# The first 1024 rows of a second Fourier mixing layer take their products with the hidden DFT matrices as seven turned block products

## Chip, cores and metric

One core of one Trainium2 chip. The metric is the device time of one execution in microseconds (us), lower is better. Of the engines, TensorE (PE) multiplies, VectorE (DVE), ScalarE (ACT) and GpSimd (POOL) work on tiles, and SyncE (SP) issues most DMAs; POOL issues the stores.

## The reference

Two mixing layers and two feed-forward layers in turn on x of 2048 rows and 512 columns, fp32, each on a layer-normed input and with a residual:

```python
def _A_ref(x, dft_seq_re, dft_seq_im, dft_hid_re, dft_hid_im):
    a = jnp.einsum("bsd,ed->bse", x, dft_hid_re)
    b = jnp.einsum("bsd,ed->bse", x, dft_hid_im)
    y = jnp.einsum("ts,bse->bte", dft_seq_re, a) - jnp.einsum("ts,bse->bte", dft_seq_im, b)
    return y

def _B_ref(x, w_gate, w_up, w_down):
    return (_gelu(x @ w_gate) * (x @ w_up)) @ w_down

x = x + _A_ref(_layernorm(x), dft_seq_re, dft_seq_im, dft_hid_re, dft_hid_im)
x = x + _B_ref(_layernorm(x), w_gate, w_up, w_down)
x = x + _A_ref(_layernorm(x), dft_seq_re, dft_seq_im, dft_hid_re, dft_hid_im)
x = x + _B_ref(_layernorm(x), w_gate, w_up, w_down)
```

The feed-forward width is 1792.

## The kernel before

**Arithmetic.** fp32 accuracy comes from splitting each operand into two fp32r tiles, hi and lo. `split` (L155) has ACT copy the source into hi (L157) and then DVE subtract hi from the source into lo (L159; for a negative operand L183 and L185). One product of 128x128 by 128x512 is then three matmuls (`mm3`, L214 to L216). The tiles of 128x512 live in 98 numbered slots (`sb`), taken in the order in which they came free; two wide tiles, `wide` (z) and `xwide` (x), can be lent out as four more slots each (`lend`).

**Layers.** Layers 0 and 2 mix (`mix`, L822), layers 1 and 3 are the feed-forward (`geglu`, L1269), done in two halves w = 0 and 1. A mixing layer multiplies first along the sequence, then by the hidden matrices wh. It works on four blocks b of 512 rows; the sequence product uses a seven-product scheme for 2 by 2 blocks, so that each block runs through stages: A11 and A12 for all four blocks first, and then for each block S2 (three interleaved chains, 24 steps of six matmuls, `six`, L988), S4 (two chains, 16 steps) and the products with wh. In S2 DVE also makes the sums of the raw DFT tiles (`make_s2`: one addition and two subtractions for every third item), in S4 one subtraction for every second.

**Products with wh.** In an unpaired block they are eight groups of four row tiles (`hid_groups`, L837; 12 matmuls a group). x is added by copying it into the four banks beforehand (`x_seeded`), and ACT copies the banks out (`x_out`). In layer 2 blocks 2 and 3 are a pair (`PAIRED`): seven forms P1 to P7, each with four operands k and two banks, six matmuls for each (`pair_product`, L910), with a prepared divided matrix wq. The result is turned, so DVE transposes it in 32 by 32 blocks and adds it into xwide or wide (`turned_into`, L812: the transpose is L815, the addition L197). For the first block of a pair P1 and P2 are done, for the second P7 and P4, and then come the twelve rest products of P6, P5 and P3 (`PAIR_REST`), which all add into one pair of banks:

```python
    def pair_rest(i):
        if sums_due:
            pair_sums()
        if i in (4, 5):
            first_sum(i - 4)
        pair_product(*PAIR_REST[i])
```

At each form's end DVE (or ACT, for P1, P2 and P7) reads the banks (`pair_ended`, L923). The operands of the forms come from `arrived` (L870) and `pair_sums` (L890, two operations of DVE for each k). For blocks 2 and 3 the twelve rest products go into the list `spare` and are taken one at a time between the products of the feed-forward layer (`beside_mix`, L1342).

**Order of the work.** All operands pass through one stream of items in the order of the products. `take` (L352) hands out the next item and splits up to seven items ahead (`AHEAD`), as far as what they are made from is there; loads run four items further (`RAW`):

```python
            if too_far(at) or make is not whole and at > n + AHEAD + stream["more"]:
                break
            if make is not whole and need and need not in cs and at > n:
                break
```

Side work is in `queue` (one at each step), `slow` (one at every few steps) and `chores` (spread over a block's products with wh; among them the norms of the next layer, `block_steps`, with their transposes at L740). A planner then orders each engine's instructions: in a planned time line it takes the ready instruction that comes first in the program. `behind` (L150) holds a split or a sum behind the newest read of a bank on its engine:

```python
    def behind(engine):
        return tc.issue_after(bank_read[engine].ins) if in_order[0] and engine in bank_read else ExitStack()
```

There are eight banks (`ps8`). DFT tiles `ws` are loaded at L337; the sums for the first two steps of block 3 are made ahead (`summed_ahead`).

Of the kernel before, what the change touches and what calls it, by code (L numbers as in the profile page):

```python
# [17 lines left out]
ND = D // P  # L18
# [25 lines left out]
MIXED = 4  # L44
PAIRED = {2: (2, 3)}
LATER = 3
LET = 5
# [6 lines left out]
def fnet_geglu(ctx: ExitStack, tc: tile.TileContext, x_in, ws, wh, wgu, wdn, wdc, whc, out):  # L54
# [409 lines left out]
    )  # L464
    PAIR_REST = [(name, k) for name in ("P6", "P5", "P3") for k in (2, 3, 0, 1)]
# [12 lines left out]
    def plan(layer):  # L478

        fore, steps = FORE[layer], []  # L480
        steps += [(b, "A11") for b in range(fore)] + [(b, "A12") for b in range(fore)]
        for b in range(NB):
            if b >= fore:
                steps += [(b, "A11"), (b, "A12")]
            if b in PAIRED.get(layer, ()):
                n = PAIRED[layer].index(b)
                steps += [(b, "S2"), (b, PAIR_EARLY[n]), (b, "S4"), (b, PAIR_LATE[n])]
            else:
                steps += [(b, "S2"), (b, EARLY_HID), (b, "S4"), (b, MID_HID), (b, LATE_HID)]
        return steps  # L490
# [23 lines left out]
    def mix_items(layer):  # L514
# [3 lines left out]
        for b, what in plan(layer):  # L518
# [17 lines left out]
            elif what == "S4":  # L536
                for i, k in skewed(2):
                    if layer and (b, k) in wss and i == 0:
                        raw(plain, wss[b, k][3])
                    elif i == 0:  # L540
                        raw(make_s4(layer, b, k), a12[k])
                    else:
                        raw(plain, a22[k])
            elif b in PAIRED.get(layer, ()):
# [277 lines left out]
    def mix(layer):  # L822
        hid, sums, chores, hid_left = {}, {}, [], [0]

        def chores_at(b):
            if b == NB - 3:
# [39 lines left out]

        paired = PAIRED.get(layer, ())
        xu, xv, pair_banks, kept_p, pair_wide, late_v, sums_due = {}, {}, {}, {}, {}, {}, []

        def arrived(b, m, c):  # L870
            if b not in paired:
                return
            t = cs.pop((m, c))
            if b == paired[0]:
                (xv if m else xu)[c] = t
                cs["P2" if m else "P1", c] = t
                return
# [19 lines left out]

        def pair_wide_load(n):
# [3 lines left out]
            moved(pair_wide[n], xs[layer, paired[n]], lambda v, rows: nc.sync.dma_start(v, rows))  # L902

        def pair_out(n):
            moved(pair_wide[n], xs[layer + 1, paired[n]], lambda v, rows: nc.gpsimd.dma_start(rows, v))

# [153 lines left out]
        def s2(b):  # L1060
            last = b == NB - 1
            if b == 0:
                lend("z")
# [39 lines left out]
        def s4(b):  # L1103
            last = b == NB - 1
            if b == NB - 4:
                sb.reclaim("z")
            if paired and b == paired[0] - 1:
                sb.reclaim("x")
# [160 lines left out]
    def geglu(w, layer):  # L1269
# [72 lines left out]
        def beside_mix(n):  # L1342
            run = spare.pop(0) if spare and (layer > 1 or n >= 1) else None
            if run:
# [62 lines left out]

        if layer == 1 and w and PAIRED:
            jobs = [weight_steps(k, whc, whd) for k in range(ND)]
            jobs = [(load, runs) for load, runs in jobs] + [(load, [run]) for load, run in map(summed_ahead, range(SUMMED))]  # L1410
# [376 lines left out]
```

## Time and profile before

| | us |
|---|---|
| three runs | 1596.59, 1596.60, 1599.89 |
| median | 1596.60 |
| span of the profiled execution | 1596.4 |
| PE busy | 1590.0 |
| DVE busy | 1169.2 |
| ACT busy | 891.6 |
| POOL busy | 294.9 |

The profile's only time for its own execution is the span, from the first to the last instruction; it stands 0.2 us below the median. The page is one execution taken by the hardware profiler. Lines such as L159 are lines of the kernel, and of a helper where a helper issues the instruction. A group of instructions is written as output<-inputs, its form, its count, its busy time and the mean length of one, and the idle time before it with what ended that. In a row of a window the columns are the stretch, its length, and for PE, PEld, DVE, ACT and POOL the busy time and in brackets the number of instructions, then the granted clock, the DMA share and GB/s. An engine's instructions overlap a little, so their mean length is more than the distance of their starts.

### The profile page before, as it was taken

The page shows a single profiled execution, that of the slowest core. Times are in us where ns is not written, and L with a number is a line of the kernel's source. Part 1 is how long each engine was busy: PE and PEld are TensorE (multiplying, and loading weights), DVE is VectorE, ACT ScalarE, POOL GpSimd, SP SyncE. Part 2 cuts the span into 40 slices and gives each one's busy share as a digit, 9 for nine tenths or more (in the row PEclk, how much of TensorE's full clock was granted, in tenths as well). Part 3 has the DMA queues.
Part 4 walks back from the last instruction along what each step waited for, and adds up shares of the span by engine and source line. Part 5 has one row for each costly group of instructions (what it writes and reads, how often), then busy time and mean ns, then how long its engine had stood idle before and what let it go on. Part 6 is the DMA issues. An engine that isn't in the chain of part 4 may idle for free.

```text
span 1596.4 us, 22835 instructions
## 1 busy us (share of the span) xinstructions
PE 1590.0 (100%) x6984; PEld 1311.2 (82%) x6984; DVE 1169.2 (73%) x2030; ACT 891.6 (56%) x1731; POOL 294.9 (18%) x505
## 2 busy tenths in 40 slices
PE   9999999999999999999999999999999999999999
PEld 6888888888888888888888888888888888888887
DVE  7997878888689794665879767778895557844574
ACT  8955465755777553666657535556553565333460
POOL 4122111251456101330040000101301000000000
PEclk9999999999999999999999999999999999999999
DMA  9898888996988999997895876878978958895445
GB/s 352 289 336 310 292 319 274 359 315 201 324 317 321 285 319 295 332 363 239 288 303 177 272 248 215 272 239 256 254 258 275 284 182 253 300 291 175 133 145 158
DMA packets 244058, 431.75 MB, mean 270 GB/s; under 512 B 29344, under 2 KB 68512, under 8 KB 242912
## 3 DMA queue, kind: packets, MB, share of 16 engines
q1 hardware_dynamic: 214128, 337.21, 66.2%
q0 software_dynamic: 27120, 90.99, 15.7%
q10 hardware_dynamic: 2688, 2.10, 0.5%
q8 instruction: 55, 0.90, 0.2%
q14 instruction: 67, 0.55, 0.1%
HBM read 341.31 MB, written 88.87 MB: 269 GB/s over the span
## 4 chain that ended last, share of the span: by engine, by line
PE 91%; issue 3%; DMA 3%; DVE 2%; ACT 1%; POOL 1%; SPq 0%; DVEq 0%; POOLq 0%; ACTq 0%
PE p L214 30%; PE p L215 30%; PE p L216 30%; DVE s L159 1%; DMA s<-ws 1%; DMA s<-t 1%; PE p L1010 0%; ACT s L157 0%; DMA s<-x 0%; DVE s L190 0%; POOL rstd L628 0%; DMA wide<-ws 0%; POOL s L754 0%; DVE xwide L190 0%; POOL wb L323 0%
## 5 line engine op out<-in xcount | busy, mean ns | idle before, releaser
L215 PE MATMUL p<-s,s 128*128 128x512 f32 x2312 | 897.4, 389 | 0.8 <-DVE s L159 0.8
L216 PE MATMUL p<-s,s 128*128 128x512 f32 x2312 | 891.8, 389 | 0.0
L214 PE MATMUL p<-s,s 128*128 128x512 f32 x2312 | 860.4, 389 | 0.3 <-ACT p L208 0.2
L157 ACT ACTIVATE s<-s 128x512 fp32r<-128x512 f32 (+1 forms) x855 | 481.3, 608 | 265.3 <-DVE s L190 73.6
L159 DVE TENSOR_TENSOR s<-s,s 128x512 fp32r<-128x512 f32 (+1 forms) x855 | 536.6, 661 | 115.3 <-ACT s L157 97.7
L215 PEld LDWEIGHTS p<-s,s 128*128 128x128 f32 x2312 | 433.9, 188 | 91.9 <-DVE s L159 1.9
L214 PEld LDWEIGHTS p<-s,s 128*128 128x128 f32 x2312 | 433.9, 188 | 91.7 <-ACT p L208 0.9
L216 PEld LDWEIGHTS p<-s,s 128*128 128x128 f32 x2312 | 434.0, 188 | 90.3
L194 DVE TENSOR_TENSOR s<-s,p 128x512 f32<-128x512 f32 x201 | 135.6, 682 | 160.3 <-PE p L216 138.1
L190 DVE TENSOR_TENSOR s<-s,s 128x512 f32<-128x512 f32 (+1 forms) x413 | 243.5, 609 | 6.2 <-DMA s<-ws 2.8
L201 ACT ACTIVATE s<-p 128x512 f32<-128x512 f32 x232 | 134.3, 593 | 108.0 <-PE p L216 106.3
L1264 ACT ACTIVATE s<-s 128x512 f32<-128x512 f32 x84 | 52.8, 628 | 46.4 <-DVE s L194 45.5
L628 POOL TENSOR_SCALAR rstd<-rstd 128x1 f32<-128x1 f32 x40 | 19.6, 489 | 237.2 <-ACT s L627 229.3
L1264 ACT ACTIVATE s<-p 128x512 f32<-128x512 f32 x28 | 16.7, 598 | 83.2 <-PE p L216 81.6
L323 POOL DMA_DIRECT2D wb<-s x84 | 46.1, 550 | 92.7 <-ACT s L157 70.5
L159 DVE TENSOR_TENSOR s<-xwide,s 128x512 fp32r<-128x512 f32 (+1 forms) x52 | 34.9, 679 | 29.2 <-ACT s L157 29.2
L651 ACT ACTIVATE s<-s,shift,rstd 128x512 f32<-128x512 f32 x59 | 47.5, 812 | 15.2 <-DVE shift L618 8.5
L1280 DVE TENSOR_TENSOR s<-s,p 128x512 f32<-128x512 f32 x56 | 38.2, 683 | 23.7 <-PE p L216 23.7
L197 DVE TENSOR_TENSOR s<-s,s 128x512 f32<-128x512 f32 (+1 forms) x71 | 42.8, 609 | 11.9 <-DMA s<-ws 10.4
L208 ACT ACTIVATE p<-p 128x512 f32<-128x512 f32 x56 | 32.6, 585 | 24.0 <-PE p L216 23.7
L157 ACT ACTIVATE s<-xwide 128x512 fp32r<-128x512 f32 (+1 forms) x52 | 31.6, 622 | 25.5 <-DVE xwide L194 18.2
L1201 POOL DMA_DIRECT2D wc<-s x42 | 30.5, 728 | 70.8 <-ACT s L157 61.9
(104 smaller groups left out, 614.9 us busy)
## 6 DMA issues: line engine op xcount, KB each, us to landing
s<-ws SPq DMA_DIRECT2D x404, 256.0 KB, 5.2
s<-wb SPq DMA_DIRECT2D x294, 256.0 KB, 5.2
s<-wc SPq DMA_DIRECT2D x182, 256.0 KB, 4.7
wb<-s POOLq DMA_DIRECT2D x98, 256.0 KB, 4.9
s<-wh SPq DMA_DIRECT2D x84, 256.0 KB, 5.3
s<-x SPq DMA_DIRECT2D x55, 256.0 KB, 5.4
wc<-s POOLq DMA_DIRECT2D x49, 256.0 KB, 5.3
xwide<-ws SPq DMA_DIRECT2D x37, 256.0 KB, 5.3
```

The lines of the kernel that those rows point to most:

```text
L157: newest["ACT"] = nc.scalar.activation(hi, src, AF.Copy)
L159: newest["DVE"] = nc.vector.tensor_tensor(lo, src, f32(hi), op=ALU.subtract)
L190: nc.vector.tensor_tensor(out, a, b, op=ALU.subtract)
L194: bank_read["DVE"] = nc.vector.tensor_tensor(out, a, b, op=ALU.add)
L197: nc.vector.tensor_tensor(out, a, b, op=ALU.add)
L201: bank_read["ACT"] = nc.scalar.activation(v, src, AF.Copy)
L214: nc.tensor.matmul(ps, ah, bh, start=start, stop=False, skip_group_check=True)
L215: nc.tensor.matmul(ps, ah, bl, start=False, stop=False, skip_group_check=True)
L216: newest["PE"] = nc.tensor.matmul(ps, al, bh, start=False, stop=stop, skip_group_check=True)
L323: nc.gpsimd.dma_start(a, f32(t))
L651: nc.scalar.activation(z, x, AF.Identity, bias=shift, scale=rstd)
L1264: nc.scalar.activation(t, g, AF.Gelu_apprx_tanh)
```

## The change

In layer 2 blocks 0 and 1 become a second pair. Their products with wh are the seven forms; the twelve rest products of this pair follow at once after block 1's other products, as a step of their own, ahead of S2 of block 2. Those of blocks 2 and 3 stay in the feed-forward layer. The x rows of blocks 0 and 1 are loaded into xwide and wide, not into banks. The wide tiles are no longer lent in S2 and S4 of block 0. The eight norms that were spread over the products of blocks 1 and 2 are now all done at block 2. `LATER` moves one early load of layer 3 by one slow step. What the diff has for layer 0 hangs on a key 0 of `PAIRED`, or on `paired` in layer 0, and there is none.

```diff
-PAIRED = {2: (2, 3)}
-LATER = 3
+PAIRED = {2: ((0, 1), (2, 3))}
+LATER = 4
...
+    def paired_with(layer, b):
+        return next((p for p in PAIRED.get(layer, ()) if b in p), ())
...
-            if b in PAIRED.get(layer, ()):
-                n = PAIRED[layer].index(b)
+            if paired_with(layer, b):
+                n = paired_with(layer, b).index(b)
                 steps += [(b, "S2"), (b, PAIR_EARLY[n]), (b, "S4"), (b, PAIR_LATE[n])]
+                if n and b < NB - 1:
+                    steps.append((b, PAIR_REST))
...
             if b == NB - 3:
                 norms, others = block_steps(layer + 1, 0)
-                later.update(norms=norms[NT:], fetches=others[:ND], others=others[ND:])
-                return norms[:NT]
+                later.update(norms=norms if b in paired else norms[NT:], fetches=others[:ND], others=others[ND:])
+                return [] if b in paired else norms[:NT]
...
-            n, early = paired.index(b), groups in PAIR_EARLY
+            pair_now[0] = by_pair[b]
+            n, early = by_pair[b].index(b), groups in PAIR_EARLY
+            if groups is PAIR_REST:
+                for i in range(len(groups)):
+                    pair_rest(i)
+                    step()
+                    for _ in range(-(-len(chores) // hid_left[0]) if chores else 0):
+                        chores.pop(0)()
+                    hid_left[0] -= 1
+                return
             if early:
                 chores.extend(chores_at(b))
-                hid_left[0] = 16 if n else 8
-                if not n:
-                    fetch_sums(paired[1])
-                pair_wide_load(n)
+                hid_left[0] = 16 if n and b == NB - 1 else 20 if n else 8
+                if b + 1 < NB:
+                    fetch_sums(b + 1)
+                pair_wide_load(b, n)
             for i, (name, k) in enumerate(groups):
-                if not early and not n and i == 2:
-                    s2_seeded(paired[1])
+                if not early and b + 1 < NB and i == (4 if n else 2):
+                    s2_seeded(b + 1)
                 pair_product(name, k)
...
-                spare.extend(lambda i=i: pair_rest(i) for i in range(len(PAIR_REST)))
+                if b == NB - 1:
+                    spare.extend(lambda i=i: pair_rest(i) for i in range(len(PAIR_REST)))
...
+            if layer and first_paired == 0 and b == FORE[layer] - 1:
+                sb.reclaim("x")
+                sb.reclaim("z")
...
-            if b == 0:
+            if b == 0 and first_paired:
                 lend("z")
                 lend("x")
```

More of the change, by code (lines that the diff above doesn't have):

```diff
@@ L464, in fnet_geglu @@
     )
-    PAIR_REST = [(name, k) for name in ("P6", "P5", "P3") for k in (2, 3, 0, 1)]
+    PAIR_REST = tuple((name, k) for name in ("P6", "P5", "P3") for k in (2, 3, 0, 1))
     def pair_items(names):
         return [(F32R, (piece(whd[k], FORM[name]),), make_pair(name, k), (name, k)) for name, k in names]
+    def paired_with(layer, b):
+        return next((p for p in PAIRED.get(layer, ()) if b in p), ())
     def skewed(n):
@@ L543, in mix_items @@
                         raw(plain, a22[k])
-            elif b in PAIRED.get(layer, ()):
+            elif paired_with(layer, b):
                 items.extend(pair_items(what))
@@ L825, in chores_at, with next_layer @@
         def chores_at(b):
+            jobs = []
+            if layer == 0 and paired and b < ND // 2:
+                two = [weight_steps(k, whc, whd) for k in range(2 * b, 2 * b + 2)]
+                jobs = [two[0][0]] + [run for i, (_, runs) in enumerate(two) for run in [load for load, _ in two[i + 1:]] + runs]
+            return jobs + next_layer(b)
+        def next_layer(b):
             if b == NB - 3:
                 norms, others = block_steps(layer + 1, 0)
-                later.update(norms=norms[NT:], fetches=others[:ND], others=others[ND:])
-                return norms[:NT]
+                later.update(norms=norms if b in paired else norms[NT:], fetches=others[:ND], others=others[ND:])
+                return [] if b in paired else norms[:NT]
             if b == NB - 2:
@@ L865, in hid_groups @@
                     x_out(layer, b * NT + i, ps)
-        paired = PAIRED.get(layer, ())
-        xu, xv, pair_banks, kept_p, pair_wide, late_v, sums_due = {}, {}, {}, {}, {}, {}, []
+        paired = {b for p in PAIRED.get(layer, ()) for b in p}
+        first_paired = min(paired, default=NB)
+        by_pair = {b: p for p in PAIRED.get(layer, ()) for b in p}
+        xu, xv, pair_banks, kept_p, pair_wide, late_v, sums_due, pair_now = {}, {}, {}, {}, {}, {}, [], [()]
         def arrived(b, m, c):
@@ L873, in arrived @@
             t = cs.pop((m, c))
-            if b == paired[0]:
+            if b == by_pair[b][0]:
                 (xv if m else xu)[c] = t
@@ L896, in pair_sums, with pair_wide_load @@
             cs["P6", c], cs["P3", c] = u, v
-        def pair_wide_load(n):
+        def pair_wide_load(b, n):
             pool = tpool if n else upool
@@ L901, in pair_wide_load @@
             pair_wide[n] = pool.tile([P, NT * D], F32, name="wide" if n else "xwide")
-            moved(pair_wide[n], xs[layer, paired[n]], lambda v, rows: nc.sync.dma_start(v, rows))
+            moved(pair_wide[n], xs[layer, b], lambda v, rows: nc.sync.dma_start(v, rows))
         def pair_out(n):
-            moved(pair_wide[n], xs[layer + 1, paired[n]], lambda v, rows: nc.gpsimd.dma_start(rows, v))
+            moved(pair_wide[n], xs[layer + 1, pair_now[0][n]], lambda v, rows: nc.gpsimd.dma_start(rows, v))
         LAST = {"P1": 3, "P2": 1, "P7": 3, "P4": 1, "P6": 1, "P5": 1, "P3": 1}
@@ L1104, in s4 @@
             last = b == NB - 1
-            if b == NB - 4:
+            if b == NB - 4 and first_paired:
                 sb.reclaim("z")
-            if paired and b == paired[0] - 1:
+            if b == first_paired - 1:
                 sb.reclaim("x")
@@ L1342, in beside_mix @@
         def beside_mix(n):
-            run = spare.pop(0) if spare and (layer > 1 or n >= 1) else None
+            run = spare.pop(0) if spare and (w == 0 or n >= 1) else None
             if run:
@@ L1408, in geglu @@
         if layer == 1 and w and PAIRED:
-            jobs = [weight_steps(k, whc, whd) for k in range(ND)]
+            jobs = [] if 0 in PAIRED else [weight_steps(k, whc, whd) for k in range(ND)]
             jobs = [(load, runs) for load, runs in jobs] + [(load, [run]) for load, run in map(summed_ahead, range(SUMMED))]
```

## The prediction, made before the changed kernel was run

> **What bounds the kernel now.** I read the busy times on the page first, then who TensorE (PE) waited for, then sums over windows, then VectorE (DVE) in order of time.
>
> ```profile
> span 1596.4 us, 22835 instructions
> PE 1590.0 (100%) x6984; PEld 1311.2 (82%) x6984; DVE 1169.2 (73%) x2030; ACT 891.6 (56%) x1731; POOL 294.9 (18%) x505
> ```
> ```profile
> PE p L1693 <- POOL ident masks.py:199: 1.4, 1, 1.4
> PE p L215 <- DVE s L159: 0.8, 1, 0.8
> PE p L214 <- ACT p L208: 0.2, 1, 0.2
> ```
> ```profile
> 30.00:880.00 850.00, 849.91 (x3750) 703.45 (x3749) 675.22 (x1220) 525.04 (x1036) 232.64 (x381) 1.00 0.88 299
> ```
>
> The columns of the last row are the stretch, its length, then busy us and count for PE, PEld, DVE, ACT and POOL, the granted clock, DMA share and GB/s. PE never rests: one matmul each 850.00/3750 = 0.2267 us at clock 1.00, and three waits, 2.4 us, in the whole run. So every matmul taken away is worth 0.2267 us, and every pause that arises is paid in full; nothing later has slack to give it back. The question is whether the other engines can feed the shorter stream.
>
> The stages of the second mixing layer are found by counting matmuls in program order (3504 come before the layer). Blocks 0, 1 and 2 whole:
>
> ```profile
> 888.90:966.20 77.30, 76.46 (x337) 62.99 (x336) 56.16 (x92) 34.02 (x61) 1.80 (x4) 1.00 0.75 253
> 966.20:1042.40 76.20, 76.20 (x338) 63.07 (x337) 54.57 (x91) 42.56 (x89) 6.89 (x14) 1.00 0.82 252
> 1042.40:1107.70 65.30, 65.30 (x290) 54.07 (x289) 48.85 (x81) 39.00 (x82) 5.65 (x12) 1.00 0.73 234
> ```
>
> Block 1 split up: S4, then the last six products with wh; and block 2's S4 and last products, a block already in the new form:
>
> ```profile
> 1004.30:1026.10 21.80, 21.80 (x98) 18.05 (x97) 10.70 (x18) 8.56 (x18) 0.74 (x2) 1.00 1.08 327
> 1026.10:1042.40 16.30, 16.30 (x74) 13.49 (x73) 16.30 (x28) 9.47 (x20) 2.86 (x5) 1.00 0.67 220
> ...
> 1077.70:1099.50 21.80, 21.80 (x97) 18.03 (x97) 14.09 (x24) 14.53 (x33) 1.26 (x4) 1.00 0.80 266
> 1099.50:1107.70 8.20, 8.20 (x38) 6.79 (x37) 8.20 (x15) 4.01 (x8) 1.26 (x3) 1.00 0.52 164
> ```
>
> DVE idles 11 us of S4 and is full (16.30 of 16.30) in the products with wh. The same in order of time, block 0 (start, us, what, idle before it and who ended that):
>
> ```profile
> 945.35 0.69 DVE L194 TENSOR_TENSOR xwide<-wide,p 128x512 f32<-128x512 f32 x1 [10.91 <-PE p L216]
> ...
> 949.43 0.69 DVE L194 TENSOR_TENSOR wide<-wide,p 128x512 f32<-128x512 f32 x1 [0.96 <-PE p L216]
> 950.11 0.69 DVE L194 TENSOR_TENSOR s<-s,p 128x512 f32<-128x512 f32 x1
> 950.71 1.89 DVE L197 TENSOR_TENSOR s<-s,s 128x512 f32<-128x512 f32 x3
> 952.52 0.69 DVE L197 TENSOR_TENSOR s<-xwide,s 128x512 f32<-128x512 f32 x1
> ```
>
> DVE stands 10.9 us before the bank read that ends S4's first sum (L194 reads p), and from S4's end it runs without a gap: splits and sums are put behind the newest bank read (the helper behind), so S4's idle time can't be used for them. Its pace: three starts from 950.71 to 952.52, 0.604 us each. In a stage S2 it owes per step six operations (plus, two minus, three splits) = 3.62 us against 18 matmuls = 4.08 us of PE. So the long products with wh of the unpaired blocks are where DVE catches up. That is the cover which the change removes.
>
> **The change, part by part.** Only the key 2 of PAIRED exists, so the branches for layer 0 are dead; wq is made where it was.
>
> *Matmuls.* Two unpaired blocks take 2 x 8 groups x 12 = 192; a pair takes 7 forms x 4 x 6 = 168. 24 fewer x 0.2267 = -5.44 us. They fall unevenly: block 0 has 48 in place of 96, block 1 has 48 and then the twelve rest products (72), which for blocks 2 and 3 lie beside the next stage and here stand bare, ahead of block 2's S2.
>
> *DVE.* Block 1 before: S2 48, S4 24, bank reads 8, splits 8 = 88 operations (the row counts 91), 53 us under 76.2. After: S2 48, S4 24, bank reads 8, splits for seven forms 8 + 12, P7 and P5 differences 8, pair sums 8, P4's end 2, first sums 6, ends of P6, P5, P3 6 + 6 + 4 = 140, so 84.6 us against 360 matmuls = 81.6 us. The turning operations' own rows, from where blocks 2 and 3 do the same work:
>
> ```profile
> L815 DVE STREAM_TRANSPOSE s<-s 128x512 f32<-128x512 f32 x6 | 4.1, 699 | 0.1
> ...
> L895 DVE SCALAR_TENSOR_TENSOR s<-s,s 128x512 f32<-128x512 f32 x4 | 2.7, 684 | 0.0
> ```
>
> They differ little from 0.684, so one price serves. Set t = 0 where PE ends P4, the last of block 1's late products. From the bank read 2.7 us before S4's end (10.9 us before t = 0) DVE owes 20 operations, 12.1 us: it is 1.2 us late. From there to the end of block 2's S2 it owes P4's end 2, sums 4, splits 10, P6 6, first sums 6, P5 6, P3 4, S2 48, its bank reads 2 = 88, 53.2 us, so it is done at 54.4 and PE one product (1.4) later, 55.8. PE's own work is 72 + 144 matmuls = 49.0 us. **By the bare count PE pauses 6.8 us.**
>
> By order it is more. P6, P5 and P3 add into one pair of banks, and DVE must read each sum before the next form may add to it. A split needs ACT's half first:
>
> ```profile
> L157 ACT ACTIVATE s<-s 128x512 fp32r<-128x512 f32 x17 | 10.3, 620 | 5.5 <-PE p L216 5.2 <-DMA s<-ws 0.3
> ```
>
> (1) DVE reads P4's banks from 1.2 to 2.4; the sum for P6's third operand is there at 3.0, ACT's half of it at 3.7, the split at 4.8, as another sum lies between. PE wants it after two products, at 2.7: pause 2.1. P6 ends at 4.8 + 2 products = 7.6. (2) DVE has split P6's fourth operand at 6.0, then seven operands that look-ahead puts before P6's bank read (P5's four, three of P3), to 10.2; the first bank is free at 10.9: pause 3.3. (3) P5's four products end at 10.9 + 5.4 = 16.4. Ahead of its bank read in DVE's order, from 11.4, stand P6's turning 4, the first sums 6, P3's last split and the first three operands of S2 (4 + 4 + 1): 20 operations, to 23.5; P3 may start at 24.3. PE can take two S2 products meanwhile (2.7), so without the wait it would be there at 19.1: pause 5.1. Sum 10.5. I take 8.5, between count and order, since PE's order is planned too and fills what it can:
>
> ```profile
> 1166.00:1198.00 32.00, 31.78 (x140) 25.86 (x139) 31.39 (x53) 19.72 (x36) 0.00 (x0) 1.00 0.72 235
> ```
> ```profile
> 1171.85 0.60 ACT L1264 ACTIVATE s<-p 128x512 f32<-128x512 f32 x1 [0.69 <-PE p L216]
> ```
>
> After block 3 DVE is full for 32 us, and PE loses only 0.2: it takes products of the feed-forward stage early (the gelu at 1171.85 reads one while the pair's products are still going), whose operands need no new DVE work. At the new place the only other work is S2 of block 2, which hangs on DVE itself.
>
> [...]
>
> *Into blocks 1 and 3.* After the shorter late products the next S2 starts with fewer operands ready. Before, block 2 into 3 does this without a pause, at a full DVE (8.20 of 8.20), though block 3's first two steps are summed ahead; block 1's are not (6 operations more, 3.6 us), and block 2 now takes eight norms in its eight groups instead of four.
>
> ```profile
> L740 DVE STREAM_TRANSPOSE wide<-s 128x512 f32<-128x512 f32 x4 | 2.8, 705 | 0.0
> ```
> ```profile
> L651 ACT ACTIVATE s<-s,shift,rstd 128x512 f32<-128x512 f32 x4 | 3.2, 808 | 0.0
> ...
> L627 ACT ACTIVATE s<-s,mean 128x512 f32<-128x512 f32 x3 | 2.1, 713 | 0.0
> L625 ACT ACTIVATE s<-s 128x512 f32<-128x512 f32 x2 | 1.2, 624 | 0.7 <-PE p L216 0.7
> ```
>
> Four norms more are four transposes, 2.8 us of DVE, and on ACT the three large operations of each, 2.1 us, which S4's idle ACT (14.53 of 21.80) can take; without that cover they hold back splits of block 3. Together 3.6 and 2.8 us of DVE against what look-ahead holds ready: 0 to 2 at each of the two places, 0.5 each taken, as the one such place on show has no pause.
>
> *Slots.* z and x are no longer lent in S2 and S4 of block 0, and block 0 no longer loads its four x rows: eight slots fewer, four needed less. There loads do wait for slots:
>
> ```profile
> SPq L337 <- DVE s L159: 19.3, 18, 3.8
> ```
> ```profile
> 906.93 0.50 PE L215 MATMUL p<-s,s 128*128 128x512 f32 x1 [0.84 <-DVE s L159]
> ```
>
> That pause (about 1.1 us) may go, with no x rows to load, or grow: -1 to +2; I take +0.5.
>
> *DMA and copies.*
>
> ```profile
> L337 SPq DMA_DIRECT2D s<-wq x28: 319/320/422, 1047.3 to 1185.5; - x28
> ```
>
> 28 loads of wq (0.32 us of SP's queue each) take the place of 32 of wh; eight x loads become eight of xwide and wide, ahead of the same late stream; eight stores stay eight on POOL's queue, later by the rest products. SP's queue gets four issues fewer, POOL's none: nothing. ACT loses eight seeds and eight copies and gains twelve halves of splits, eight copies and seeds of the forms, in stages where it is under 60% busy: nothing; without that cover 0.6 us each. LATER moves one look-ahead load by one slow step: nothing, as no row shows a wait for it.
>
> Sum: -5.44 + 8.5 + 0.5 + 0.5 + 0.5 = +4.6 us on the profiled span of 1596.4, which stands 0.2 under the runs' median of 1596.6: 1601.
>
> **The rivals.**
> *Bare count.* The planner packs DVE without loss, the other places cost nothing: -5.4 + 6.8 = +1.4, 1598; with half of it recovered 1595. For it: DVE shows no gap once loaded (950 to 966). Against: three chains through one pair of banks.
> *The turning slips.* (the other side) 18 of the 88 (first sums 6, the turning of P6, P5 and P3 4 each) feed stores that nobody needs before block 2's norms. If the order has 11 or more of them behind S2, in S4 of block 2, where DVE is idle for 7.7 us (14.09 of 21.80), the count's pause of 6.8 goes, and from 3 on it is under the gain of 5.4: 1591 to 1593. Against: after block 3 DVE takes such work among its splits at once and does not put it off, and the turned operands of later S2 steps come after it in the program.
> *Loads starve.* Rest operands and S2's operands share the slots with the z parts, all alive in block 1 while block 3 has freed part of them; loads wait for products that are themselves paused, 5 us more: 1605 to 1610. For it: the 19.3 us of slot waits above. Against: blocks 2 and 3 run on the same slots without a pause.
> *The clock.* The trace shows clock 1.00 over the pause at 906. Should matmuls run at twice 0.2267 after pause (3) for as long as it lasted (5 us, 11 matmuls), that adds 2.5: 1604. [...]
>
> **How the numbers follow.** Likeliest, pauses of 8 to 13 us with the small terms: 0.46, 1599 to 1605, named at 1601. Bare count 0.27, 1595 to 1599. Turning slips 0.17. Loads starve 0.07, clock 0.03. A change of 0.2% (3.2 us) is about what can be told from none: faster 0.17, same 0.27, slower 0.56. The range 1592 to 1606 leaves out the ends of the first and last, under 0.2.
>
> **What would show it.** 24 fewer matmuls. Right: pauses of PE inside the twelve rest products and at the start of block 2's S2, ended by DVE (L159 splits, and L194, the bank reads), DVE without a gap from block 1's late products to deep in S2, the rest of the layer as before. Wrong: PE at 0.2267 through the rest products (then the order has the turning late), or pauses elsewhere: in block 0's S2 ended by loads, in block 3's S2 ended by ACT.

## The result and the profile after

| | before | after |
|---|---|---|
| median of four runs, us | 1597.32 | 1636.05 |
| lowest to highest | 1596.59 to 1599.89 | 1635.49 to 1637.06 |
| span of the profiled execution | 1596.4 | 1633.9 |

The changed kernel is slower: ratio 1.0236, interval 1.0215 to 1.0258. The forecast of 1601 had the side right and the size wrong, by a factor of eight: +37.5 us on the span instead of +4.6.

The page's busy times of the changed kernel, and below them who PE waited for (us in total, times, longest):

```profile
span 1633.9 us, 22846 instructions
PE 1600.2 (98%) x6960; PEld 1308.7 (80%) x6960; DVE 1201.7 (74%) x2082; ACT 896.2 (55%) x1735; POOL 299.6 (18%) x505
```
```profile
PE p L214 <- ACT s L157: 11.2, 8, 2.8
PE p L215 <- DVE s L159: 7.4, 6, 3.3
PE p L214 <- DVE s L194: 4.1, 2, 3.9
PE p L214 <- ACT s L183: 3.9, 2, 2.5
```

24 matmuls are gone, yet PE is busy 10 us longer: some of them ran slower. The waits of PE were 1 us on operands before; now splits (L157, L159, L183) and bank reads (L194) hold it 26.6 us. Three windows of the second mixing layer follow (columns as in the prediction: length, then busy us and count for PE, PEld, DVE, ACT, POOL, then granted clock, DMA share, GB/s). The first is blocks 0 and 1, the second the twelve rest products and block 2, the third block 3 and the first products of the feed-forward layer.

```profile
887.60:1022.30 134.70, 132.07 (x578) 107.53 (x577) 105.93 (x174) 60.85 (x109) 1.08 (x2) 1.00 0.71 211
1022.30:1129.90 107.60, 93.29 (x380) 71.46 (x379) 87.00 (x144) 53.34 (x112) 12.89 (x21) 0.97 0.75 224
1129.90:1213.40 83.50, 73.45 (x289) 56.86 (x289) 65.09 (x107) 43.76 (x85) 20.60 (x39) 0.92 0.80 233
```

Length less count x 0.2267 is what a stretch loses: 3.7, 21.5 and 18.0 us. Outside the layer nothing is lost against before. So there are two large holes, and the second one, in block 3, begins 87 us after the last of the new rest products has started (1048.9 and 1136.0 us). On average DVE is full in neither: 87.00 of 107.60 and 65.09 of 83.50. It was full at the start of block 2's S2:

```profile
1045.00:1065.00 20.00, 16.13 (x65) 11.23 (x64) 20.00 (x34) 7.60 (x13) 2.77 (x5) 1.00 0.42 130
```

So DVE's time was short for a stretch. Over the whole of the two holes it was its order and what it waited for.

The clock, which before stood at 1.00 throughout the layer, was halved in four stretches:

```profile
1029.30:1036.00 6.70, 5.63 (x13) 4.02 (x14) 3.95 (x7) 1.17 (x2) 0.00 (x0) 0.50 0.48 157
1138.40:1141.80 3.40, 3.40 (x8) 2.10 (x8) 3.40 (x7) 3.40 (x7) 2.30 (x5) 0.50 0.64 204
1169.20:1172.50 3.30, 3.16 (x8) 2.48 (x9) 1.33 (x3) 3.21 (x7) 0.00 (x0) 0.50 1.02 263
1199.90:1206.70 6.80, 5.79 (x13) 4.16 (x14) 6.80 (x12) 4.24 (x7) 0.00 (x0) 0.50 0.20 74
```

Matmuls in them start 0.427 us apart instead of 0.227. Of the 43.5 us lost, 9.1 are slow clock (what the matmuls in these stretches lose beside the pauses) and 34.4 pauses. The first stretch in order of time, on PE and then on DVE:

```profile
1026.35 0.73 PE L214 MATMUL p<-s,s 128*128 128x512 f32 x2 [1.04 <-ACT s L157]
1030.37 0.79 PE L215 MATMUL p<-s,s 128*128 128x512 f32 x1 [3.29 <-DVE s L159]
1030.96 0.63 PE L216 MATMUL p<-s,s 128*128 128x512 f32 x1
1031.39 0.63 PE L215 MATMUL p<-s,s 128*128 128x512 f32 x1
```
```profile
1024.81 2.49 DVE L159 TENSOR_TENSOR s<-s,s 128x512 fp32r<-128x512 f32 x4
1027.22 0.68 DVE L909 SCALAR_TENSOR_TENSOR s<-s,s 128x512 f32<-128x512 f32 x1
1027.83 0.68 DVE L159 TENSOR_TENSOR s<-s,s 128x512 fp32r<-128x512 f32 x1
1028.43 0.68 DVE L909 SCALAR_TENSOR_TENSOR s<-s,s 128x512 f32<-128x512 f32 x1
1029.03 2.67 DVE L159 TENSOR_TENSOR s<-s,s 128x512 fp32r<-128x512 f32 x4
```

PE has the hi of P6's third operand at 1026.35 and waits 3.3 us for its lo, which comes in the last group: DVE runs without a gap, but its order has other splits and two pair sums (L909) first. In the whole of the second window PE waited for:

```profile
PE p L215 <- DVE s L159: 6.7, 5, 3.3
PE p L214 <- ACT s L157: 4.6, 4, 1.5
PE p L214 <- ACT s L183: 2.5, 1, 2.5
PE p L214 <- DVE s L194: 0.2, 1, 0.2
```

### The profile page after: what moved, and what is told of

It reads as the page before. It is cut to its first block, busy times and chain, and to the rows that moved or that the text cites. A ratio compares the mean times of both kernels' runs of the same rounds, so it can differ in the third digit from the quotient of the medians.

```text
span 1633.9 us, 22846 instructions
## 1 busy us (share of the span) xinstructions
PE 1600.2 (98%) x6960; PEld 1308.7 (80%) x6960; DVE 1201.7 (74%) x2082; ACT 896.2 (55%) x1735; POOL 299.6 (18%) x505
## 4 chain that ended last, share of the span: by engine, by line
PE 90%; DVE 4%; DMA 3%; ACT 1%; issue 1%; SPq 0%; DVEq 0%; ACTq 0%
PE p L215 30%; PE p L214 30%; PE p L216 30%; DMA s<-ws 2%; DVE s L159 1%; DVE s L190 1%; DMA s<-x 1%; PE p L1034 1%; ACT s L157 1%; DVE s L197 1%; DVE s L820 0%; DVE s L194 0%; DMA s<-wq 0%; ACT s L632 0%; ACT s L630 0%
## 5 line engine op out<-in xcount | busy, mean ns | idle before, releaser
L157 ACT ACTIVATE s<-s 128x512 fp32r<-128x512 f32 (+1 forms) x889 | 502.3, 608 | 322.4 <-DVE s L190 92.1
L159 DVE TENSOR_TENSOR s<-s,s 128x512 fp32r<-128x512 f32 (+1 forms) x889 | 558.6, 664 | 118.1 <-ACT s L157 101.7
L214 PEld LDWEIGHTS p<-s,s 128*128 128x128 f32 x2304 | 433.5, 189 | 117.6 <-ACT s L157 17.4
L194 DVE TENSOR_TENSOR s<-s,p 128x512 f32<-128x512 f32 x213 | 143.8, 682 | 191.8 <-PE p L216 154.1
L190 DVE TENSOR_TENSOR s<-s,s 128x512 f32<-128x512 f32 (+1 forms) x432 | 255.8, 614 | 15.5 <-DMA s<-ws 12.8
L197 DVE TENSOR_TENSOR s<-s,s 128x512 f32<-128x512 f32 (+1 forms) x77 | 46.7, 616 | 18.3 <-DMA s<-ws 13.2
L633 POOL TENSOR_SCALAR rstd<-rstd 128x1 f32<-128x1 f32 x40 | 22.9, 572 | 181.5 <-ACT s L632 173.8
L1307 DVE TENSOR_TENSOR s<-s,p 128x512 f32<-128x512 f32 x56 | 38.3, 683 | 22.7 <-PE p L216 21.0
L919 POOL DMA_DIRECT2D x<-wide x8 | 5.2, 657 | 242.7 <-DVE s L197 172.6
L1307 DVE TENSOR_TENSOR s<-s,s 128x512 f32<-128x512 f32 x56 | 38.5, 688 | 1.3
```

What stands on the lines that cost most here:

```text
L157: newest["ACT"] = nc.scalar.activation(hi, src, AF.Copy)
L159: newest["DVE"] = nc.vector.tensor_tensor(lo, src, f32(hi), op=ALU.subtract)
L190: nc.vector.tensor_tensor(out, a, b, op=ALU.subtract)
L194: bank_read["DVE"] = nc.vector.tensor_tensor(out, a, b, op=ALU.add)
L197: nc.vector.tensor_tensor(out, a, b, op=ALU.add)
L214: nc.tensor.matmul(ps, ah, bh, start=start, stop=False, skip_group_check=True)
```

## The experiments

Each kernel was run once, beside a run of the kernel before on the same chip. Those runs of the kernel before lie between 1596.1 and 1598.9, so differences in time under 3 us are not read. The table is the yardstick for all: us lost to pauses and slow clock by stage of layer 2, each matmul's distance from the one before beyond 0.2267 us, summed over the matmuls of the stage. "Start" is blocks 0 and 1, "middle" the rest products and block 2, "end" block 3 and the first products of layer 3.

| kernel | time | start | middle | end |
|---|---|---|---|---|
| before | 1597.3 | 1.1 | 0.0 | 0.6 |
| after | 1636.1 | 4.0 | 21.5 | 18.0 |
| x1_no_rest | 1614.5 | 8.5 | 8.3 | 17.4 |
| x2_norms_s4 | 1634.1 | 7.3 | 28.4 | 4.4 |
| x3_kept2 | 1627.2 | 4.1 | 11.9 | 15.1 |
| x4_no_turn | 1621.1 | 5.8 | 7.2 | 17.8 |
| y1_single | 1602.4 | 0.9 | 0.0 | 0.8 |
| y2_pair01 | 1626.8 | 9.5 | 17.6 | 2.7 |
| y3_wide_late | 1635.8 | 3.6 | 21.8 | 17.7 |
| y4_norms_noact | 1627.8 | 5.6 | 19.7 | 11.6 |
| z1_padded | 1660.8 | 5.6 | 23.6 | 19.1 |
| z2_ahead3 | 1634.0 | 8.7 | 18.7 | 15.6 |
| z3_raw8 | 1632.2 | 6.6 | 24.9 | 10.2 |
| z4_combo | 1630.0 | 4.6 | 6.8 | 22.8 |
| n1_padded_norest | 1629.8 | 7.1 | 2.0 | 19.2 |
| n2_single_norms8 | 1617.1 | 1.0 | 0.0 | 16.6 |
| n3_combo_noact | 1615.2 | 1.7 | 8.4 | 6.9 |
| n4_kept_s4 | 1628.6 | 5.5 | 20.7 | 6.5 |
| n5_norms8_no_wide | 1610.1 | 1.1 | 0.0 | 8.5 |
| n6_norms8_no_act | 1608.4 | 0.0 | 0.1 | 7.5 |

Not in the table: x1, y1, n1, n2, n5 and n6 lose 3 to 6 us in layer 3, and x3, z4, n3 and n4 lose 5 to 7 us in layer 0.

### One part at a time

The first theory was the prediction's, drawn out: the new rest products overload DVE and the debt is carried to the end of the layer. The rival: the eight norms at block 2.

**x1_no_rest** drops the step:

```diff
-                if n and b < NB - 1:
-                    steps.append((b, PAIR_REST))
...
```

> The twelve rest products of blocks 0 and 1, with their sums, splits, bank reads and turning, are left out (72 matmuls, 16.3 us of TensorE); the rest is the changed kernel. Overload theory (VectorE cannot do the rest products' work in their time, and all later pauses follow from being late): the pauses from 1024 us on go, TensorE waits under 8 us in the layer, 1583 to 1590 us. Norms theory (the pauses after 1065 us come from the eight norms now put at block 2): some 20 us of pauses and slow clock stay at blocks 2 and 3, 1600 to 1608 us.

Neither theory was met. 16.3 us of matmuls are gone with the products and the time falls by 21.5; the middle falls from 21.5 to 8.3, the end stays at 17.4. The end is not the rest products' debt.

**x2_norms_s4** moves the norms:

```diff
-                hid_left[0] = 16 if n and b == NB - 1 else 20 if n else 8
+                hid_left[0] = 16 if b >= NB - 2 else 20 if n else 8
...
-                    if last and paired:
+                    if b in paired and b >= NB - 2:
                         for _ in range(-(-len(chores) // hid_left[0]) if chores else 0):
```

> The eight norms at block 2 are spread over its S4 steps and products (two in the early products, six in S4) instead of its eight products; the computation is whole. Norms theory: the waits of TensorE on ScalarE at 1099 to 1102 and 1134 to 1142 us (3 and some 4 us, one slow clock period) go, and what follows shrinks: 1622 to 1630 us. Overload theory: under 4 us, 1632 to 1637 us.

The time is in the overload theory's range and says the wrong thing: the loss has moved, the end from 18.0 down to 4.4 and the middle from 21.5 up to 28.4. Where the norms stand decides where it is lost.

**x3_kept2** and **x4_no_turn** lighten DVE in the middle: sums of block 2 kept from layer 0, and the first pair's sixteen turning operations left out.

```diff
-KEPT = ((0, 0), (0, 1), (0, 2))
+KEPT = ((0, 0), (0, 1), (0, 2), (2, 0), (2, 1), (2, 2), (2, 3))
```
```diff
-                    turned_into(pair_wide[1], c + 2 * (name == "P5"), to[c])
+                    if pair_now[0][0]:
+                        turned_into(pair_wide[1], c + 2 * (name == "P5"), to[c])
```

(and the same at the other two calls of `turned_into`)

> The sums of the raw DFT tiles for the first four steps of block 2 are stored in layer 0 and only loaded and split in layer 2: 16 operations of VectorE fewer (9.7 us) right behind the rest products, the computation is whole. Overload theory: the pauses between 1041 and 1065 us (some 9 us) go and with them half of those behind: 1612 to 1624 us. Norms theory: only those 9 us at most, 1627 to 1632. Late loads theory (the loads come late for their slots whatever VectorE does): 1633 to 1638.

> The turning of the first pair's results into the wide tiles (8 transposes and 8 additions of VectorE, 9.7 us) is left out, all products stay. Overload theory: pauses between 1035 and 1065 us shrink by up to 9 us and later ones with them: 1615 to 1626 us. Norms theory: 1627 to 1632. Late loads theory: 1633 to 1638.

x4 is in the overload theory's range: with 9.7 us of DVE's work gone (16 x 0.604) the middle falls by 14.3, nearly all of it in block 2, which becomes free of pauses; the rest products themselves still lose 7.2. x3 is at the low end of the other range: the middle falls by 9.6, the end by 2.9, and 5.1 us are lost anew in layer 0, where the kept sums are written. Both leave the end at 15 to 18.

### Which half, and which way

**y1_single** is the changed code with the old pair alone, **y2_pair01** has the new pair alone:

```diff
-PAIRED = {2: ((0, 1), (2, 3))}
+PAIRED = {2: ((2, 3),)}
```
```diff
-PAIRED = {2: ((0, 1), (2, 3))}
+PAIRED = {2: ((0, 1),)}
...
```

(In y2 two conditions that go by the second pair change with it.)

> The changed kernel's code with blocks 2 and 3 alone as a pair: all other edits of the change stay. If they cost nothing: 1594 to 1599 us. If one of them (the wide tiles not lent, LATER) carries part of the loss: above 1600.

> Blocks 0 and 1 alone as a pair, blocks 2 and 3 unpaired (so as many matmuls as before the change; norms still all at block 2). Two causes theory (rest products and block 2's S2 one, norms with the second pair's wide tile the other): pauses up to 1065 us as in the changed kernel, some 20 us, and under 4 us behind: 1613 to 1621 us. Knock-on theory (once late, the layer stays late): pauses of 15 us and more at blocks 2 and 3, 1628 to 1640.

y1's time fell in the range for a cost, but in layer 2 it loses no more than before does; its 4 us lie at 1366 to 1375 us, in layer 3, and the changed kernel does not have them. So the code that is left of the change costs nothing in layer 2. Other than its expectation says, not all other edits stay in y1: with `first_paired` at 2 it lends the wide tiles in block 0 again, and its norms stand four and four again. In y2 the middle loses 17.6 with the old pair undone: that hole belongs to the new pair. The end loses only 2.7, though all eight norms stand at block 2 there too; blocks 2 and 3 have their long products again, and no x is loaded into `wide`. Its time fell between the two theories.

**y3_wide_late** and **y4_norms_noact** try two ways by which norms could act: the late load of block 3's x into `wide`, and the norms' operations on ScalarE (left out, with those on GpSimd, for layer 3's first half, which is then not normalized).

```diff
-                pair_wide_load(b, n)
+                if b < NB - 1:
+                    pair_wide_load(b, n)
...
                 if b == NB - 1:
+                    pair_wide_load(b, n)
                     spare.extend(lambda i=i: pair_rest(i) for i in range(len(PAIR_REST)))
```
```diff
-                z = normed(layer, r0 + i, True)
+                z = row_of(layer, r0 + i, True) if layer == 3 and w == 0 else normed(layer, r0 + i, True)
```

> Both pairs; the load of block 3's x rows into wide is issued after block 3's last product instead of before its S4; nothing else. Collision theory (eight norms keep wide until 1143 us, so this load of 512-byte pieces falls beside S4's loads, which then take 9.7 us): the pauses at 1166 to 1182 us go and those at 1196 to 1206 shrink, 1622 to 1629 us. Order theory (the pauses of block 3 come from an order planned for other times): 1631 to 1638.

> The eight norms at block 2 keep their loads, transposes and stores, but ScalarE's operations for them are left out (rows are turned without being normed). If ScalarE's norms hold back the splits: the pauses at 1099 to 1102 and 1134 to 1142 us go (7 us), wide is free some us sooner: 1620 to 1629 us. If the loads of the norms or the collision behind them cause it: 1630 to 1637.

y3 told nothing, though it looked like a verdict. The load on the chip, in the changed kernel and in y3 (SP's issues: median ns, first and last start):

```profile
L916 SPq DMA_DIRECT2D wide<-x x4: 371/576/729, 1149.8 to 1154.5; - x4
```
```profile
L916 SPq DMA_DIRECT2D wide<-x x4: 371/740/871, 1149.7 to 1154.2; - x4
```

The program has the load elsewhere, but on the chip it had not moved, so y3 tests nothing. y4 met its range (1620 to 1629), with the end at 11.6.

### Is it PE's time, or the look-ahead?

The next theory: the long products with wh are a stock from which DVE lives, and the change spends it. **z1_padded** gives PE that time back without work for the others; **z2_ahead3** and **z3_raw8** look further ahead in layer 2, z2 with the splits (second diff), z3 with the loads, by four items; **z4_combo** joins both, by three items each, to kept sums of four steps in each of blocks 1 and 2.

```diff
                 mm3(ps[c], (w[:, half[0]][:, cut], w[:, half[1]][:, cut]), (hi, lo), FIRST.get(name) == k, LAST[name] == k)
+                if pair_now[0][0] == 0 and name in ("P1", "P2", "P7", "P4"):
+                    mm3(ps[c], (w[:, half[0]][:, cut], w[:, half[1]][:, cut]), (hi, lo), False, LAST[name] == k)
```
```diff
+DEEPER = 3
...
+            if layer:
+                stream["more"] = DEEPER
```

> Each of the sixteen block products of the first pair that stand in blocks 0 and 1 (P1, P2, P7, P4) is multiplied twice, so its sums are not the reference's: 96 more matmuls (21.8 us), and no more work for VectorE, ScalarE or the loads. If the pauses come because the shortened products with wh of blocks 0 and 1 no longer give VectorE and ScalarE time to get ahead of TensorE (stock theory): pauses and slow clock of layer 2 fall from 43.5 us to 5-15, so 1636 + 21.8 - (28 to 38) = 1619-1630. If the norms that wait at block 2, or local orders, make them: they stay at 36-46, so 1650-1660.

> From S2 of layer 2's first block on, operands are split up to ten products ahead instead of seven. If the depth of the look-ahead is what keeps VectorE from using its idle time (14.4 us busy of 20 at 1065-1085 and 1085-1105 us): 1610-1627. If VectorE's and ScalarE's planned order and the late loads are the limit: 1630-1640.

> From S2 of layer 2's first block on, the loads of operands run eight products ahead of the splits instead of four. If the single loads of ws that land 8.7 and 9.7 us after their issue hold up VectorE's line: about 5 pauses go, 1618-1630. If VectorE's and ScalarE's time is short whenever the loads land: 1632-1640.

> Three changes together: the ws sums of the first four steps of S2 in blocks 1 and 2 are kept in layer 0 and loaded (24 fewer sums for VectorE, less than in x3_kept2 at one place, more at another), ten products of look-ahead, and loads seven ahead. Stock theory: each gives part of the stock back, 1598-1617. If only the kept sums act, as in x3_kept2 (1627): 1618-1630.

The stock theory fell: z1 is 24.7 us slower for 21.8 us of matmuls, with the middle at 23.6 and the end at 19.1. z2 and z3 are in the rival's ranges. z4 stands at the edge of the poorer range, but its middle is down to 6.8, and its end, up at 22.8, shows the norms at work. Waits from 1110 to 1175 us in z4:

```profile
POOL rstd L634 <- ACT s L633: 20.3, 3, 13.6
...
PE p L215 <- ACT s L158: 11.5, 4, 5.2
...
DVE wide L746 <- ACT s L657: 9.2, 4, 3.0
ACT shift L636 <- POOL rstd L635: 9.0, 3, 5.2
```

A norm goes ACT (L631 to L633), POOL (two operations on 128x1), ACT (L636, L657), DVE (the transpose, L746). While ACT waits 9.0 us in it for POOL, the splits behind it in ACT's line (L158 in z4) wait too, and PE waits for splits. The longest of these waits, 5.2 us, stands behind a POOL operation on 128x1 that is recorded with 6.12 us; the next one of its kind has 0.19. Why is not shown.

### The norms alone, and the rest products alone

**n1_padded_norest** is x1 and z1 together; **n2_single_norms8** is y1 with all eight norms at block 2; **n3_combo_noact** is z4 with y4's edit; **n4_kept_s4** is x2 and x3 together.

```diff
-                later.update(norms=norms if b in paired else norms[NT:], fetches=others[:ND], others=others[ND:])
-                return [] if b in paired else norms[:NT]
+                later.update(norms=norms if layer else norms[NT:], fetches=others[:ND], others=others[ND:])
+                return [] if layer else norms[:NT]
```

> As x1_no_rest (the twelve rest products of the first pair with their VectorE work left out), and each of the sixteen products of that pair in blocks 0 and 1 multiplied twice, so that TensorE has as many matmuls as with the pair of blocks 2 and 3 alone. If TensorE's time at the end of block 1 is what VectorE needs to get ahead, and the rest products only use that stock up: blocks 2 and 3 run as in y1_single, pauses and slow clock under 8 us, 1600-1608. If the eight norms at block 2 make the pauses by themselves: x1_no_rest's 34 us stay, 1614.5 + 21.8 = 1630-1640.

> As y1_single (only blocks 2 and 3 paired, 1602.4), but all eight norms of layer 3's first half stand at block 2 of layer 2, as in the changed kernel, instead of four at block 1 and four at block 2. If the norms' place is a cause by itself: pauses in block 2's late products and in block 3, 1610-1625. If it only hurts where the stock is gone: 1600-1606.

> As z4_combo (1630.0, kept sums in blocks 1 and 2, deeper look-ahead, earlier loads), and the norms' operations on ScalarE and GpSimd for layer 3's first half are left out (their transposes on VectorE stay), so that half is not normalized. z4_combo's 18.8 us in S2 of block 3 stand where ScalarE waits for GpSimd inside norms. If both causes together make the whole: 1600-1612. If the pauses only move: 1618-1630.

> Keeps the result: the ws sums of four steps of block 2 kept in layer 0 (x3_kept2, 1627), and two norms in block 2's early products and six in its S4 (x2_norms_s4, 1634). If the two causes add: x3's pauses in block 3 and at the start of layer 3 (14.8 us) go as they did in x2, and x2's in S4 and P2 of block 2 (13.5 us) go half with the kept sums: 1609-1620. If the pauses only move: 1624-1634.

n2 is the cleanest run of the study: without any of the new products it loses 16.6 us at the end and nothing in the middle. y1 loses 0.8 at the end. The norms' place is a cause by itself, as n2's first range had it. Blocks 3 of y1 and of n2:

```profile
1111.20:1178.70 67.50, 67.29 (x296) 55.10 (x295) 60.63 (x101) 38.75 (x71) 17.42 (x32) 1.00 0.92 260
```
```profile
1110.60:1193.70 83.10, 71.87 (x295) 57.53 (x294) 64.22 (x107) 41.17 (x78) 19.70 (x36) 0.92 0.80 240
```

The same 295 matmuls take 15.6 us more. In n1 the middle is clean (2.0) and the end keeps 19.2: its time is at the edge of the second range, but each theory was right for one hole. Without rest products, PE's time in blocks 0 and 1 does count (8.3 in x1, 2.0 here); with them it does not (23.6 in z1). n3 ended between its ranges, with 7.4 us of its time lost in layer 0. n4 gives 1628.6: as in x2, pauses only move while the norms stand in the middle. No kernel with the first pair came near the one before.

### How eight norms reach block 3

**n5_norms8_no_wide** is n2 with block 3's x not loaded; **n6_norms8_no_act** is n2 with y4's edit.

```diff
+            if b == NB - 1:
+                nc.gpsimd.memset(pair_wide[n], 0.0)
+                return
             moved(pair_wide[n], xs[layer, b], lambda v, rows: nc.sync.dma_start(v, rows))
```

> As n2_single_norms8 (1617.1), and block 3's rows of x are not loaded into the tile wide (GpSimd fills it with zeros), so they are not added. If the late load of wide (1135.7-1138.8 us, 1112 in y1_single) holds up the loads of ws behind it, and these the splits: the pause of 6.5 us at P4 and the slow clock near it go, 1607-1611. If the norms' operations or the planned order make the pauses: 1615-1618.

> As n2_single_norms8 (1617.1), and the norms' operations on ScalarE and GpSimd for layer 3's first half are left out (their loads and their transposes on VectorE stay), so that half is not normalized. If these operations hold up ScalarE's line: the norms end earlier, the load of wide moves forward to about 1115 us, and 1602-1608. If the eight transposes and the loads at block 2 alone are enough: 1612-1618.

n5 met the load's range, n6 missed the upper end of its own by 0.4 us. The load in y1, n2 and n6:

```profile
L916 SPq DMA_DIRECT2D wide<-x x4: 337/478/482, 1112.2 to 1113.7; - x4
```
```profile
L916 SPq DMA_DIRECT2D wide<-x x4: 337/608/740, 1135.7 to 1138.0; - x4
```
```profile
L916 SPq DMA_DIRECT2D wide<-x x4: 337/484/496, 1113.5 to 1114.9; - x4
```

The norms gather their transposes in the tile `wide`, and block 3's x is loaded into the same tile, so the load waits until the last norms have been stored from it. In n2 it goes out 23 us late, into a stretch where the loads of ws are wanted. The chain that ends at 1162 us in n2 runs from that store over the load to one load of ws, which takes 11.59 us:

```profile
1127.73 7.93 DMA t<-wide
...
1135.68 7.79 DMA wide<-x
...
1145.18 11.59 DMA s<-ws
```

SyncE's queue itself stands 4.6 us for the four loads of x to land before it issues more of ws (0.4 in n6, nothing in y1). The loads of ws take (DMA issues from 1130 to 1165 us, KB each, median us to landing; n2, then n6):

```profile
s<-ws SPq DMA_DIRECT2D x12, 256.0 KB, 9.2
```
```profile
s<-ws SPq DMA_DIRECT2D x11, 256.0 KB, 5.5
```

This median alone would not show it: it is 6.0 in n5 and 7.1 in y1, which has no such pause. But ACT, in n2, stands before its splits until ws lands, and PE behind it:

```profile
1150.81 2.20 ACT L157 ACTIVATE s<-s 128x512 fp32r<-128x512 f32 x4 [3.37 <-DMA s<-ws]
1156.85 1.67 ACT L157 ACTIVATE s<-s 128x512 fp32r<-128x512 f32 x3 [3.85 <-DMA s<-ws]
```
```profile
1159.10 1.22 PE L214 MATMUL p<-s,s 128*128 128x512 f32 x2 [6.12 <-ACT s L183]
```

Take the load away (n5), or the norms' operations, so that the load moves back to 1113.5 (n6), and this pause with its slow clock is gone: 16.6 falls to 8.5 and 7.5. What is left there is for the larger part one pause at the first product of layer 3, 4.1 us in n5 and 3.4 in n6, with about 1 us of slow clock after it.

In the changed kernel the load was never moved by itself, so the shares are not shown there. Its pauses in block 3 and at the first product of layer 3:

```profile
1138.18 2.97 PE L214 MATMUL p<-s,s 128*128 128x512 f32 x6 [1.82 <-ACT s L157]
...
1169.34 0.80 PE L214 MATMUL p<-s,s 128*128 128x512 f32 x1 [2.84 <-ACT s L157]
...
1179.91 0.73 PE L214 MATMUL p<-s,s 128*128 128x512 f32 x2 [1.38 <-ACT s L183]
...
1200.91 0.80 PE L214 MATMUL p<-s,s 128*128 128x512 f32 x1 [3.93 <-DVE s L194]
```

The first three end on ACT's splits; behind the third stands a load of ws that took 9.73 us. The fourth is 4.09 us beyond the usual distance in after, x1, x4, y3, y4, n1, n2 and n5 alike, and x2 does not have it. DVE's line in the changed kernel shows what it is:

```profile
1196.57 1.28 DVE L194 TENSOR_TENSOR s<-s,p 128x512 f32<-128x512 f32 x2 [4.84 <-PE p L216]
1197.77 0.68 DVE L190 TENSOR_TENSOR s<-s,s 128x512 f32<-128x512 f32 x1
1198.37 1.29 DVE L159 TENSOR_TENSOR s<-s,s 128x512 fp32r<-128x512 f32 x2
1199.58 0.68 DVE L190 TENSOR_TENSOR s<-s,s 128x512 f32<-128x512 f32 x1
1200.18 0.68 DVE L194 TENSOR_TENSOR s<-s,p 128x512 f32<-128x512 f32 x1
```

S4's last matmul starts at 1196.6, and the bank read that PE waits for is DVE's seventh operation from there, behind two other bank reads, two differences and two splits. The same seven stand in x1 and n5, and in n6, where the pause is 3.41. So this pause is DVE's order; why the planner sets it so, and what another order would give, was not tested.

## Why the prediction was wrong

*Matmuls.* 6984 to 6960, -5.44 us: right.

*Rest products and block 2, 8.5 us.* The place was right, and the cause in part: PE waits inside the rest products and in S2 of block 2, for DVE's splits 6.7 us and for ACT's halves 7.1 (4.6 and 2.5), and taking work from DVE (x4) clears block 2, though not the rest products, which still lose 7.2. Bank reads, on which the working put 8.4 of its 10.5 us, hardly count: 0.2. The term was mis-sized: 15.6 us in the stages it named (8.1 in the rest products, 7.5 in S2), and 5.9 more in S4 and the late products of block 2, 21.5 in all. Two steps failed. The three pauses worked out by hand were ordered wrongly: that at P6's third operand, given 2.1, came as two, 1.2 and 3.5, with 2.9 of slow clock behind them, while those for the shared banks, given 3.3 before P5 and 5.1 before P3, were 0.3 each. And the debt was closed at the end of S2 by counting DVE's operations as if each ran when its turn came. They did not: in S2 of block 2 DVE stood 5.5 us before a subtraction whose tile of ws landed late, with the split that PE wanted behind it, and PE paused 1.5 us there.

```profile
1083.95 0.69 DVE L190 TENSOR_TENSOR s<-s,s 128x512 f32<-128x512 f32 x1 [5.53 <-DMA s<-ws]
```

*Into blocks 1 and 3, 0.5 us each, bounds 0 to 2.* This is the step that failed most. Block 1 lost 2.5; block 3 and the first products of layer 3 lost 18.0, and n2, without any new product, loses 16.6 there. The prediction priced four more norms by their busy time (2.8 us of DVE, 2.1 of ACT) and found cover for it. Busy time was not the price. They hold a tile that a later load needs: 8.1 of n2's 16.6 us go when that load goes (n5). Their chain runs ACT, POOL, ACT inside ACT's line (from 1022 to 1215 us ACT waits 3.8 us for POOL in it), and it is ACT's splits that PE waits for in block 3 (1.82, 2.84 and 1.38 us). The sign that the prediction named for being wrong, pauses in block 3's S2 ended by ACT, came with the 1.82 us at 1138.18. At the first product of layer 3, 4.09 us more are DVE's order. The prediction had the load's side in hand, "eight x loads become eight of xwide and wide, ahead of the same late stream", and put it at nothing: it did not ask when `wide` comes free.

*Slots, +0.5.* S2 of block 0 went from 1.1 to 1.6 us: right.

*DMA and copies, nothing.* Right by the count of issues, wrong by the place of the load, as above.

*The rivals.* Bare count and slipping turning ops did not come: DVE did not put the turning off, and x4 shows that it hurt where it stood. Starving loads named the kind of wait, but for the slots and in the wrong place. The clock rival, at 0.03 and +2.5 us, came true within the others: 9.1 us. That matmuls would run at twice 0.2267 us was an assumption, which no trace from before shows between products; in the changed kernel they start 0.427 us apart in the slow stretches, which last 3.4 or 6.8 us. "Every pause that arises is paid in full" held: of the 37.5 us, 2.9 + 21.5 + 17.4 are losses beyond those of before, less 5.44; 1.1 us remain unassigned.

## What to carry to other kernels

When a change moves side work, follow the tiles that this work holds and ask when each comes free and which load waits for it. Here moving four norms alone (n2) cost 16.6 us, more than three times the 4.9 us of their own busy time, in a stage whose own work stayed the same, and 8.1 of it went with one load. In lines that run in order, count a stage's operations only as a lower bound: here one late load of ws stopped DVE for 5.5 us with the wanted split behind it, and in z4 three waits for POOL stopped ACT for 9.0 us with splits behind them, so idle time in an engine's average did not show that it had time to spare when it counted. And before reading an experiment on an order, look in its trace whether the order moved at all.

## What the hardware showed

The clock fell after shorter pauses than the 5 us of the prediction's clock rival. All slow stretches but those at the program's two ends last 3.41 us or a multiple (6.83, 3.41, 3.41 and 6.83 in the changed kernel), and their starts lie on a grid: in the changed kernel 1029.2, 1138.4, 1169.1 and 1199.8 us are 32, 9 and 9 steps of 3.413 apart. Laying that grid over the twenty traces and adding up all of PE's pauses in each step: at full clock, all 61 steps with more than 2.08 us of pauses were followed by a step at half clock, none with less than 2.06 was, and between these both happened. Once slow, a step with 1.09 us or more kept the clock down (29 of 29), one with 0.97 or less freed it. In the changed kernel the steps ahead of the four falls hold 2.96, 2.26, 2.78 and 3.02 us of pauses, and no other step of the layer at full clock more than 1.79; two slow steps, with 1.34 and 1.51, were followed by a slow one, and four, with at most 0.36, were not. So a pause of 1 us alone in its step was not followed by a fall in these traces. Each of the four falls in the changed kernel cost 1.6 to 2.9 us more.
